# Attention by hash buckets and experts on one Trainium2 core: GpSimd's residuals wait for more of VectorE's subtractions, and the projection's table is loaded first

## The chip, the cores and the metric

The kernel runs on one core of a Trainium2 chip. The metric is the device time of one execution in microseconds (us). Engines are named as the profile names them: PE is TensorE (PEld its weight loads), DVE is VectorE, ACT is ScalarE, POOL is GpSimd, SP is SyncE, which here only issues DMAs. ACTq and SPq are the queues of DMA issues on ACT and SP.

## The reference

Four batches, eight heads, 768 positions, 64 channels per head. Each query and key gets a six-bit bucket from the signs of a projection, and a query attends only to keys of its bucket. Then each batch's 128 best rows by a gate score go through one expert.

```python
q_bits = (np.einsum('bhsd,dk->bhsk', q, proj) > 0)
k_bits = (np.einsum('bhsd,dk->bhsk', k, proj) > 0)
mask = q_bucket[:, :, :, None] == k_bucket[:, :, None, :]
scores = np.where(mask, scale * np.matmul(q, k.transpose(0, 1, 3, 2)), -1e9)
attn = np.exp(scores - max) ; attn = attn / (attn.sum(-1) + 1e-9)
x = (attn @ v) with the heads side by side, per batch [768, 512]
# expert: scores = x @ w_gate; the top 128 rows of each batch:
h = np.maximum(xe @ w1, 0.0)
out[b, top_idx] = xe + sigmoid(scores) * (h @ w2)
```

## The kernel before, in words

There are 32 heads (4 batches of 8), handled one after the other in a pipeline, and 16 pairs of heads, since a 128-partition tile holds two heads of 64 channels. Every number is kept as a high part in 16 bits and a low part, the residual, also in 16 bits, so that matrix products in 16-bit types come out near float32.

For a pair, `load_x` brings queries and keys (tiles X), `split_xh` (ACT) writes the high part into the tile T, `split_xl` (DVE, L500) the low part, and SP moves halves of T into the operands A and B of the two heads. `hash_half` multiplies X by the projection's table `pjt` (PE, L463) for two pairs at a time, `signs` turns the result into plus and minus values on DVE (L480), writes them to the tile `sg`, and then takes the difference of its two halves (L487; GpSimd for the first group, DVE for the seven others). SP moves the signs into A too. `load_v`, `split_vh` (ACT, L548) and `split_vl` (DVE, L554) do the same for the values: the low part of V. For the very last head, `score_v`, `score_vh` and `score_vl` (DVE, L576, 128x6 elements) add a column to V that makes its gate score; `sum_v`, `sum_lo` (DVE, L615) and `seed` make sums of V that start each head's accumulator.

For a head, `max_unit` (PE, L669), `max_relu` (ACT, L677) and `max_red` (DVE, L686, tiles mj and M) find each query's largest bucket match, 12 products of 128x384 per head in four PSUM banks that are handed round (`pmax.take`, `pmax.give`): a bank comes free when the engine that reads it is done. `st_unit` (PE, L720 with A and L724 with B) makes nine tiles of scores, `st_exp` (ACT, L738 and L740) their exponentials P in float32. The residual of P, tile R, is `r_chunk`: of the three key groups of a head, GpSimd takes group 1 in even heads, groups 0 and 2 in odd heads (L758, 128x1536 elements, 46 of them), and DVE the others in halves (L755, 128x768, 100 of them). `av` (PE, L774) multiplies high part and residual of P by V: for each of 36 blocks two weight loads of P and one of R. `recip` and `norm` (DVE, L784 to L796) divide.

The expert's weights are loaded and split between all this: ACT casts (L833), GpSimd subtracts (L835, 128x512, 16 of them). Expert products are L992 and L1016, their inputs turned by L957 and split by L965 and L1006.

The order of all of it is written out by hand: the table ORDER lists, one number per step, which step emits its instructions next. Each engine runs its own instructions in that order and waits on semaphores for what it needs from others. Besides these waits for data, there is one of another kind. A step on DVE that is wrapped in `mine` notes itself as the last one that used the path to SBUF which DVE and GpSimd share; a GpSimd step wrapped in `turn` waits, when it is emitted, until the DVE instruction noted at that moment is done. All 62 of GpSimd's residuals and weight subtractions (46 and 16) are wrapped in `turn`. On DVE L500, L563, L659, L755 and L857 are wrapped in `mine`; L487, L554 and L576 are not.

```python
    def mine(i):
        st["port"] = i
```

At the start `init_first` (L290) issues the first loads: half of the last pair's keys on ACT's queue (L292), of its queries on SP's queue (L293), and the table `pjt`, 128 rows of 276 bytes, on ACT's queue (L294). These become head 0. `negate` (ACT, L389) changes the sign of some columns of the table, `split_first` (ACT, L392) writes the high parts, `hash_first` (PE, L400) the projection, and the signs follow on ACT (L415, L416) and DVE (L410). `keep_warm` (PE, L311) issues products whose result nobody reads.

Of the kernel before, what the change touches and what calls it, by code (L numbers as in the profile page):

```python
# [16 lines left out]
ALU = mybir.AluOpType  # L17
# [226 lines left out]
def body(ctx, tc, qk, v, pj, wg, w1, w2, cst, out):  # L244
    nc = tc.nc
# [15 lines left out]
    pjt = cp.tile([P, PJW], F32, name="pjt")  # L261
# [27 lines left out]

    def init_first():  # L290
        xa = sb.tile([P, 2, S], F32, tag="P", name="Xa", bufs=4)
        nc.scalar.dma_start(xa[D:P, 1], qk[NP - 1, 1][D:P])  # L292
        nc.sync.dma_start(xa[D:P, 0], qk[NP - 1, 0][D:P])  # L293
        nc.scalar.dma_start(pjt, pj)  # L294
        nc.vector.memset(oneb, 1.0)
        nc.scalar.activation(oneb, oneb, AF.Copy)
        nc.gpsimd.memset(ones16, 1.0)
        nc.vector.memset(AA[0][0:D].bitcast(F32), 0.0)
        st["xa"] = xa
# [59 lines left out]
    def mine(i):  # L359
        st["port"] = i  # L360
# [9 lines left out]
    def need(*keys):  # L370

        assert all(k in st for k in keys), keys
# [97 lines left out]
    def signs(g, e):  # L470
        hp = st["hp", g, e]
        if ("sg", g) not in st:
            st["sg", g] = sb.tile([P, S // 2 + S], F16, tag="sg", name=f"sg{g}", bufs=2)
        if g > 1:
            need(("ps", 4 * g - 4))
        for j in range(2):
            st["sgd", 2 * g + j, e] = True
        t = st["sg", g]
        sd, sg = t[:, : S // 2], t[:, S // 2 :]
        nc.vector.tensor_scalar(  # L480
            sg[:, e * 384 : (e + 1) * 384], hp[:, :384], pjt[:, 66:67], pjt[:, 67:68],
            op0=ALU.is_gt, op1=ALU.mult,
        )
        pmax.give(f"hp{g}_{e}")
        if e:
            eng = nc.vector if g else nc.gpsimd
            eng.tensor_tensor(sd, sg[:, 0:384], sg[:, 384:768], op=ALU.subtract)  # L487

    def split_xh(p, r):
        if ("T", p) not in st:  # L490
# [59 lines left out]
    def split_vl(pr):  # L550
        need(("vh", pr))
        st["vl", pr] = True
        t, vv = st["V", pr], V[pr % NV].rearrange("p c h d -> p (c h) d")
        nc.vector.scalar_tensor_tensor(  # L554
            vv[:, :, VL : VL + D], t.rearrange("p c h d -> p (c h) d"), VS, vv[:, :, :D],
            op0=ALU.mult, op1=ALU.subtract,
        )

    def score_v():
        need(("vh", NH // 2 - 1))  # L560
# [12 lines left out]

    def score_vl():
        need("gvh")
        nc.vector.scalar_tensor_tensor(  # L576
            V[VLAST][:, :, 1, VL + D + 1 : VL + OW], st["gv"], VS, V[VLAST][:, :, 1, D + 1 : OW],
            op0=ALU.mult, op1=ALU.subtract,
        )
        st["gvl"] = True  # L580

    def sum_v(g):
# [634 lines left out]
    def begin():  # L1217
        init_first()
        keep_warm(0, WARM[0])
        negate()  # L1220
        split_first(1)
        split_first(0)
        low_first(1)
        hash_first()
        keep_warm(1, WARM[1])
# [15 lines left out]
    for g in range(NH // 4):  # L1241
        for e in range(2):
            at(hash_half, g, e)
            at(signs, g, e)
    for fn in (score_v, score_vh, score_vl):
        at(fn)
# [4 lines left out]
    for h in range(NH):  # L1251
# [15 lines left out]
        if h % 2 == 0:  # L1267
            for fn in (load_v, split_vh, split_vl):
                at(fn, h // 2)
            g, k = GROUP[h // 2]  # L1270
            if k == len(SUMS[g]) - 1:
                for fn in (sum_v, sum_hi, sum_lo, seed_row, seed_keep):
                    at(fn, g)
# [92 lines left out]
```

## Time and profile before

| | |
|---|---|
| median of 3 runs | 395.42 us (393.97 to 396.38) |
| the profiled execution | 395.86 us, of which the span of instructions is 393.8 us |
| PE busy | 376.2 us, 96% of the span |
| DVE busy | 346.6 us, 88% |
| ACT busy | 313.8 us, 80% |
| POOL busy | 180.0 us, 46% |
| mean granted clock of TensorE | 0.986 |

The span is counted from the first to the last instruction; times in the rows are from its start. Busy means that the engine has an instruction under way, even where that instruction itself stands and waits for a path to memory: such a stall lengthens the instruction's row and leaves no idle time. A row of the timeline gives start, duration, engine, line, operation, and in brackets the idle time before it with what ended it. Neighbouring rows of one engine overlap by up to 0.1 us, since each counts its own filling and draining.

### The profile page before, as it was taken

What the parts mean: (1) busy time and instruction counts of PE and PEld (TensorE: products, weight loads), DVE (VectorE), ACT (ScalarE), POOL (GpSimd) and SP (SyncE); (2) the same over time, 40 slices, a digit from 0 to 9 for tenths busy, and PEclk for the clock granted to TensorE, in tenths of its full rate; (3) what the DMA queues carried; (4) which work ended last, traced back from release to release, by engine and by line L of the source; (5) the groups of instructions that cost most, each with busy time, mean ns of one, the idle gap of its engine ahead of it and who ended that gap; (6) DMA issues with size and microseconds to landing.
All of it is one profiled execution on the core that took longest, in us unless ns stands there. A gap on an engine that the chain in (4) does not pass through costs nothing.

```text
span 393.8 us, 14144 instructions
## 1 busy us (share of the span) xinstructions
PE 376.2 (96%) x5736; PEld 274.5 (70%) x5746; DVE 346.6 (88%) x935; ACT 313.8 (80%) x665; POOL 180.0 (46%) x103
## 2 busy tenths in 40 slices
PE   6789999999999999799999999999999999899995
PEld 4346777677666777488657777676677788577894
DVE  3889999999799989979899899999999989989742
ACT  6899999899898998778588889988988986665210
POOL 8135567574736265724434444444326364220113
PEclk8799999999999999989999999999999999999999
DMA  7477667676776554633745543757464433010311
GB/s 236 139 196 230 176 197 221 181 220 165 221 206 166 138 156 125 199 95 106 233 117 185 142 132 91 204 148 199 100 173 110 103 67 112 2 42 2 108 30 53
DMA packets 26353, 56.37 MB, mean 143 GB/s; under 512 B 4218, under 2 KB 10942, under 8 KB 26288
## 3 DMA queue, kind: packets, MB, share of 16 engines
q1 hardware_dynamic: 15792, 36.89, 35.7%
q10 hardware_dynamic: 9824, 16.49, 12.9%
q0 software_dynamic: 672, 2.10, 1.7%
q8 instruction: 45, 0.74, 0.8%
q14 instruction: 20, 0.16, 0.1%
HBM read 26.58 MB, written 7.35 MB: 86 GB/s over the span
## 4 chain that ended last, share of the span: by engine, by line
PE 73%; DVE 9%; issue 7%; ACT 5%; DMA 2%; POOL 1%; POOLq 0%; ACTq 0%; SPq 0%; DVEq 0%
PE av L774 23%; PE st L720 14%; PE bank L669 14%; PE st L724 13%; PE bank L992 3%; DVE mj L686 2%; PE bank L463 2%; PE bank L1016 2%; ACT me L677 2%; DMA A<-sg 2%; DVE R L755 1%; DVE V L554 1%; ACT P L738 1%; DMA pjt<-in_pj_dram 1%; DVE sg L487 1%
## 5 line engine op out<-in xcount | busy, mean ns | idle before, releaser
L758 POOL TENSOR_TENSOR R<-P 128x1536 f16<-128x1536 f32 x46 | 134.2, 2919 | 136.4 <-ACT P L738 24.2
L774 PEld LDWEIGHTS <-P 128*128 128x128 bf16 x2304 | 126.3, 98 | 26.2 <-issue 0.8
L774 PE MATMUL av<-V,P 128*128 128x65 f16 (+2 forms) x2304 | 133.6, 193 | 0.1
L774 PE MATMUL av<-V,R 128*128 128x65 f16 (+1 forms) x1152 | 126.7, 193 | 0.0
L738 ACT ACTIVATE P<-st 128x512 f32<-128x512 f32 x192 | 111.8, 598 | 17.6 <-PE av L774 9.3
L720 PE MATMUL st<-A 128*128 128x512 f16 (+1 forms) x384 | 119.5, 326 | 1.4 <-ACT P L738 1.2
L724 PE MATMUL st<-B 128*128 128x512 f16 (+1 forms) x384 | 118.9, 326 | 0.7 <-ACT B L432 0.7
L686 DVE CUSTOM_DVE_ANT_0 mj<-bank,me 128x384 bf16<-128x384 f32 x192 | 102.4, 550 | 18.1 <-ACT me L677 9.0
L669 PE MATMUL bank<-A 128*128 128x384 f16 x384 | 108.7, 330 | 7.7 <-DVE W L615 2.0
L774 PEld LDWEIGHTS <-R 128*128 128x128 f16 x1152 | 106.2, 98 | 0.0
L677 ACT ACTIVATE me<-bank 128x384 f32<-128x384 f32 x192 | 92.2, 491 | 17.5 <-DVE M L686 8.0
L755 DVE TENSOR_TENSOR R<-P 128x768 f16<-128x768 f32 x100 | 94.1, 960 | 0.5 <-ACT P L738 0.2
L740 ACT ACTIVATE P<-st 128x512 f32<-128x512 f32 x96 | 56.9, 596 | 2.2 <-PE st L724 0.7
L669 PEld LDWEIGHTS <-A 128*128 128x128 f16 x384 | 34.8, 98 | 25.1 <-issue 5.6
L724 PEld LDWEIGHTS <-B 128*128 128x128 f16 x384 | 37.6, 98 | 18.0 <-issue 2.5
L720 PEld LDWEIGHTS <-A 128*128 128x128 f16 x384 | 37.5, 98 | 15.8 <-issue 2.5
L500 DVE SCALAR_TENSOR_TENSOR T<-X,T 128x768 f16<-128x768 f32 x32 | 31.6, 997 | 0.0
L493 ACT ACTIVATE T<-X 128x768 f16<-128x768 f32 x32 | 26.6, 841 | 0.6 <-DMA B<-T 0.6
L835 POOL TENSOR_TENSOR w2l<-W,w2h 128x512 bf16<-128x512 f32 x8 | 11.2, 1400 | 17.8 <-DVE R L755 12.5
L835 POOL TENSOR_TENSOR w1l<-W,w1h 128x512 bf16<-128x512 f32 x8 | 13.0, 1630 | 12.7 <-ACT w1h L833 6.5
L554 DVE SCALAR_TENSOR_TENSOR V<-V,V 128x768 f16<-128x768 f32 x16 | 17.8, 1114 | 0.3 <-ACT V L548 0.2
L796 DVE TENSOR_TENSOR x<-av,rc 128x384 f32<-128x384 f32 x32 | 17.7, 553 | 0.2
(142 smaller groups left out, 412.8 us busy)
## 6 DMA issues: line engine op xcount, KB each, us to landing
X<-in_qk_dram SPq DMA_DIRECT2D x32, 384.0 KB
B<-T SPq DMA_DIRECT2D x62, 192.0 KB
A<-T SPq DMA_DIRECT2D x31, 240.0 KB
V<-in_v_dram ACTq DMA_DIRECT2D x16, 384.0 KB
out_dram<-x ACTq DMA_DIRECT2D x6, 768.0 KB
W<-in_w_dram ACTq DMA_DIRECT2D x8, 512.0 KB
sbc<-scores SPq DMA_DIRECT2D x3, 384.0 KB
A<-sg SPq DMA_DIRECT2D x31, 31.5 KB
```

Source lines behind the costliest of these rows:

```text
L493: nc.scalar.activation(st["T", p][:, o : o + S], st["X", p, r], AF.Copy, scale=XS)
L500: mine(nc.vector.scalar_tensor_tensor(t[:, o : o + S], st["X", p, r], XS, t[:, i : i + S], op0=ALU.mult, op1=ALU.subtract))
L669: nc.tensor.matmul(pt[:, :384], a[0][:, t * P : (t + 1) * P], a[1][:, 384:768] if i else K[h % NA], start=True, stop=True,)
L677: nc.scalar.activation(me, st["mx", h, t, 0][:, :384], AF.Relu)
L686: nc.vector.tensor_tensor_reduce(out=jk, in0=st["mx", h, t, 1][:, :384], in1=st["me", h, t], op0=ALU.add, op1=ALU.max, scale=1.0 / MS, sca ...
L720: nc.tensor.matmul(pt[:, o : o + n], a[1][:, c * P : (c + 1) * P], a[0][:, q0 : q0 + n], start=True, stop=False,)
L724: nc.tensor.matmul(pt[:, o : o + n], bt[:, 0, c * P : (c + 1) * P], bt[:, 1, q0 : q0 + n], start=False, stop=True,)
L738: nc.scalar.activation(pp[:, r, 0:512], pt, AF.Exp, scale=ES)
L740: nc.scalar.activation(pp[:, :, 512:768], pt.rearrange("p (a b) -> p a b", a=2), AF.Exp, scale=ES)
L755: mine(nc.vector.tensor_tensor(t[:, r], pp[:, r], hi_view(pp, r), op=ALU.subtract))
L758: turn(nc.gpsimd.tensor_tensor(t, pp, hi_view(pp, a), op=ALU.subtract))
L774: nc.tensor.matmul(o[:, t, :n], l, vv[:, c, hh, v0 : v0 + n], start=False, stop=last and l is lo, skip_group_check=True,)
```

## The change

Three DVE instructions are wrapped in `mine` as well: the difference of the signs (L487), the low part of V (L554) and the low part of the last head's score column (L576). A GpSimd instruction wrapped in `turn` that is emitted after one of them now waits for it. And the table `pjt` is loaded by SP's queue, ahead of all else on it, where ACT's queue loaded it as its second. ORDER is the same.

```diff
     def init_first():
         xa = sb.tile([P, 2, S], F32, tag="P", name="Xa", bufs=4)
+        nc.sync.dma_start(pjt, pj)
         nc.scalar.dma_start(xa[D:P, 1], qk[NP - 1, 1][D:P])
         nc.sync.dma_start(xa[D:P, 0], qk[NP - 1, 0][D:P])
-        nc.scalar.dma_start(pjt, pj)
...
         if e:
-            eng = nc.vector if g else nc.gpsimd
-            eng.tensor_tensor(sd, sg[:, 0:384], sg[:, 384:768], op=ALU.subtract)
+            if g:
+                mine(nc.vector.tensor_tensor(sd, sg[:, 0:384], sg[:, 384:768], op=ALU.subtract))
+            else:
+                nc.gpsimd.tensor_tensor(sd, sg[:, 0:384], sg[:, 384:768], op=ALU.subtract)
...
-        nc.vector.scalar_tensor_tensor(
+        mine(nc.vector.scalar_tensor_tensor(
             vv[:, :, VL : VL + D], t.rearrange("p c h d -> p (c h) d"), VS, vv[:, :, :D],
             op0=ALU.mult, op1=ALU.subtract,
-        )
+        ))
...
-        nc.vector.scalar_tensor_tensor(
+        mine(nc.vector.scalar_tensor_tensor(
             V[VLAST][:, :, 1, VL + D + 1 : VL + OW], st["gv"], VS, V[VLAST][:, :, 1, D + 1 : OW],
             op0=ALU.mult, op1=ALU.subtract,
-        )
+        ))
```

Following `mine` and `turn` through ORDER, 14 of the 62 GpSimd instructions find another DVE instruction noted than before. For ten of them it is one that neither they nor a GpSimd instruction ahead of them waited for: the weight subtraction before R_0_1609, and the residuals R_0_2085, R_2_2668, R_0_3552, R_2_3713, R_0_5115, R_0_5596, R_1_5964, R_1_6369 and R_0_7649 (the last number only tells tiles apart). R_2_2668 and R_2_3713 get to wait for a difference of signs, R_0_7649 for the score column, the seven others for a low part of V. The order on PE, DVE and POOL is the same row by row, but for line numbers, which grow by two.

SP's queue at the start, before and after (A_90 and Xa belong to head 0, X to the next pairs):

```order
L1359 UNCONDITIONAL_BRANCH
L293 DMA Xa<-in_qk_dram 64x768
L378 DMA X_1_163<-in_qk_dram 128x768
L378 DMA X_0_165<-in_qk_dram 128x768
L378 DMA X_1_167<-in_qk_dram 128x768
```

```order
L1361 UNCONDITIONAL_BRANCH
L292 DMA pjt<-in_pj_dram 128x69
L294 DMA Xa<-in_qk_dram 64x768
L378 DMA X_1_163<-in_qk_dram 128x768
L378 DMA X_0_165<-in_qk_dram 128x768
L378 DMA X_1_167<-in_qk_dram 128x768
```

The table has come in front of every load of SP's queue, and all of them stand one place later.

POOL's waits around R_2_2668, before and after (semaphores of other engines by name; DVE_49 is VectorE's, Pool_49 GpSimd's own, DMAHW1_49 a load's):

```order
L835 TENSOR_TENSOR w2l<-W_2328,w2h 128x512 [waits DMAHW1_49,DVE_49,Activation_49]
L758 TENSOR_TENSOR R_0_2618<-P_0_2497 128x1536 [waits DVE_49,Activation_49]
L758 TENSOR_TENSOR R_2_2668<-P_2_2489 128x1536 [waits Activation_49,Pool_49]
L835 TENSOR_TENSOR w2l<-W_2328,w2h 128x512
L758 TENSOR_TENSOR R_1_2826<-P_1_2759 128x1536 [waits DVE_49,Activation_49,Pool_49]
```

```order
L837 TENSOR_TENSOR w2l<-W_2328,w2h 128x512 [waits DMAHW1_49,DVE_49,Activation_49]
L760 TENSOR_TENSOR R_0_2618<-P_0_2497 128x1536 [waits DVE_49,Activation_49]
L760 TENSOR_TENSOR R_2_2668<-P_2_2489 128x1536 [waits DVE_49,Activation_49,Pool_49]
L837 TENSOR_TENSOR w2l<-W_2328,w2h 128x512
L760 TENSOR_TENSOR R_1_2826<-P_1_2759 128x1536 [waits DVE_49,Activation_49,Pool_49]
```

R_2_2668 now also waits for DVE. At most of the ten places DVE_49 stood there before, and only the count that is waited for has grown.

DVE's rows around the score column, where R_0_7649 and R_2_7679 run on POOL (the same before and after; V_96<-gv is the score column, V_96<-V_6538 the last pair's low part):

```order
L686 ISA mj_2_7624,M_85<-bank_67,me_2_7514 128x384
L686 ISA M_85 128x1
L576 SCALAR_TENSOR_TENSOR V_96<-gv,V_96 128x6
L686 ISA mj_3_7651,M_85<-bank_67,me_3_7626 128x384
L686 ISA M_85 128x1
L796 TENSOR_TENSOR x_6636<-av_7423,rc_7606 128x6x64
L686 ISA mj_5_7677,M_85<-bank_64,me_5_7426 128x384
L686 ISA M_85 128x1
L554 SCALAR_TENSOR_TENSOR V_96<-V_6538,V_96 128x12x64
```

R_0_7649 now waits for the third row. The last row is emitted after both residuals, so neither waits for it, before or after.

## Rows read from the trace of the kernel before

**Rows 1.** The page's first part: busy time of each engine

```profile
PE 376.2 (96%) x5736; PEld 274.5 (70%) x5746; DVE 346.6 (88%) x935; ACT 313.8 (80%) x665; POOL 180.0 (46%) x103
```

**Rows 2.** Waits of PE: engine, line, waited for: us in total, times, longest

```profile
PE bank L669 <- DVE W L615: 2.0, 1, 2.0
...
PE bank L669 <- DVE M L686: 1.7, 2, 1.2
```

**Rows 3.** The page's part 5 (first row), then a source view: ns min/median/max

```profile
L500 DVE SCALAR_TENSOR_TENSOR T<-X,T 128x768 f16<-128x768 f32 x32 | 31.6, 997 | 0.0
...
L487 DVE TENSOR_TENSOR sg<-sg x7: 358/477/2845, 43.3 to 285.8; 128x384 f16<-128x384 f16 x7
```

**Rows 4.** Timeline of DVE, 162 to 167 us: start, duration, instruction

```profile
163.59 2.85 DVE L487 TENSOR_TENSOR sg<-sg 128x384 f16<-128x384 f16 x1
166.36 0.48 DVE L615 SCALAR_TENSOR_TENSOR W<-WH,cs,bank 128x260 f16<-128x260 f16 x1
```

**Rows 5.** Timeline of POOL, whole span

```profile
118.26 5.57 POOL L758 TENSOR_TENSOR R<-P 128x1536 f16<-128x1536 f32 x2 [3.05 <-DVE rc L784]
123.79 1.16 POOL L835 TENSOR_TENSOR w2l<-W,w2h 128x512 bf16<-128x512 f32 x1
...
163.48 2.74 POOL L758 TENSOR_TENSOR R<-P 128x1536 f16<-128x1536 f32 x1
...
261.93 2.77 POOL L758 TENSOR_TENSOR R<-P 128x1536 f16<-128x1536 f32 x1 [3.68 <-ACT P L738]
...
332.01 2.75 POOL L758 TENSOR_TENSOR R<-P 128x1536 f16<-128x1536 f32 x1 [5.58 <-DVE rc L784]
336.10 2.75 POOL L758 TENSOR_TENSOR R<-P 128x1536 f16<-128x1536 f32 x1 [1.34 <-ACT P L740]
```

**Rows 6.** Windows: stretch, us, busy of PE, PEld, DVE, ACT, POOL, clock, DMA share

```profile
164.86:166.89 2.03, 0.00 (x0) 0.00 (x0) 1.98 (x2) 0.51 (x2) 1.36 (x1) 1.00 0.81 237
168.04:171.45 3.41, 3.41 (x29) 2.70 (x28) 2.89 (x9) 2.45 (x6) 0.00 (x0) 0.50 0.39 127
171.45:175.00 3.55, 3.55 (x78) 3.24 (x76) 2.64 (x5) 3.00 (x8) 1.20 (x1) 1.00 0.02 5
```

**Rows 7.** Timeline of DVE, 330 to 341.5 us

```profile
333.49 1.31 DVE L576 SCALAR_TENSOR_TENSOR V<-gv,V 128x6 f16<-128x6 f32 x1
334.71 0.55 DVE L686 CUSTOM_DVE_ANT_0 mj<-bank,me 128x384 bf16<-128x384 f32 x1
...
336.13 3.54 DVE L554 SCALAR_TENSOR_TENSOR V<-V,V 128x768 f16<-128x768 f32 x1
```

**Rows 8.** Timeline of PE, 338 to 342 us

```profile
340.20 0.32 PE L669 MATMUL bank<-A 128*128 128x384 f16 x1 [1.21 <-DVE M L686]
340.80 0.38 PE L1016 MATMUL bank<-w2h,hth 128*128 128x512 f16 x1 [0.28 <-DVE htl L1006]
```

**Rows 9.** Timeline of all engines and DMA queues, 0 to 14 us

```profile
0.75 0.56 ACTq L292 DMA_DIRECT2D Xa<-in_qk_dram  x1
0.75 0.58 SPq L293 DMA_DIRECT2D Xa<-in_qk_dram  x1
...
1.35 0.60 ACTq L294 DMA_DIRECT2D pjt<-in_pj_dram  x1
...
4.95 0.22 ACT L389 ACTIVATE pjt<-pjt 128x18 f32<-128x18 f32 x1 [1.47 <-DMA pjt<-in_pj_dram]
5.19 1.57 ACT L392 ACTIVATE A<-Xa 64x768 f16<-64x768 f32 x2
```

**Rows 10.** Timeline of DVE, 118 to 126 and 261 to 262.2 us

```profile
120.73 0.49 DVE L487 TENSOR_TENSOR sg<-sg 128x384 f16<-128x384 f16 x1
...
123.87 1.89 DVE L500 SCALAR_TENSOR_TENSOR T<-X,T 128x768 f16<-128x768 f32 x1
...
261.14 0.96 DVE L554 SCALAR_TENSOR_TENSOR V<-V,V 128x768 f16<-128x768 f32 x1 [0.16 <-ACT V L548]
```

**Rows 11.** Timeline of PE's weight loads, 337.5 to 343 us

```profile
338.42 0.10 PEld L774 LDWEIGHTS <-R 128*128 128x128 f16 x1
```

## The prediction

> **What bounds the kernel now.** I read the page's busy times first: PE works 376.2 of 393.8 us [rows 1], so whatever shortens the kernel must remove idle time of PE or lie ahead of its first or behind its last product. Then the waits of PE, which say what its idle time is for. Apart from the start two rows stand out [rows 2]: 2.0 us in one piece before a product of L669, ended by DVE's L615, and 1.7 us in two pieces before L669, ended by DVE's L686. None of the fourteen rows of that view names a residual of GpSimd. So DVE is late in a few places, and the question is why.
>
> The source views answer it. The difference of signs takes 358 ns at best and 2845 ns at worst [rows 3]. The long one runs from 163.59 to 166.44, and GpSimd's residual from 163.48 to 166.22 [rows 4, 5]: it began 0.11 us earlier, and DVE's instruction ended just after it. DVE stood for it, 2.49 us. L615 follows it, and the bank that L615 reads is the one for which PE waits: in 164.86 to 166.89 PE does nothing. From 168.04 to 171.45, after that idle time, the granted clock is 0.50, 1.2 instead of 2.4 GHz, with PE busy throughout; before and after it is 1.00 [rows 6].
>
> The same is seen near the end. The score column begins at 333.49 under a residual that began at 332.01, and takes 1.31 us [rows 5, 7]. The residual had 1.27 us to go, so at most that is standing. At 336.13 the last pair's low part of V begins, 0.03 us after the next residual, and takes 3.54 us where another low part took 0.96 [rows 5, 7, 10]: 2.58 us. PE then idles 1.21 and 0.28 us for DVE [rows 8].
>
> **The change part by part.** Nothing is computed more or less. The sum is made against the profiled execution, 395.86 us, which is 0.44 us above the median of the runs, 395.42.
>
> *The sign difference at 163.59.* R_2_3713 will wait for it. It then takes its 0.36 us and ends at 163.95, and L615 at about 164.4, before PE comes to the product that needs it (164.86). The 2.03 us of idle time go. If the half clock goes with them, PE does the work of 3.41 us in half the time, 1.70 us less. Both together are 3.7, the first alone 2.0. Between them DVE decides: its own work after L615 is only released by PE's product, so it gains 2.0 us there, and in the window of the half clock it is busy 2.89 of 3.41 us [rows 6], so it can make up 0.5 us in that window and 0.9 (3.55 less 2.64) in the next, and 3.4 us is all it can have gained by 175 us. I take 3.1, between this and the 2.0. What is put behind the wait: R_2_3713 starts at about 164.1 (0.16 us from DVE's end to GpSimd's start, an estimate from the places where GpSimd waits for DVE now) instead of 163.48, and ends at 166.9. PE needs it first at 171.06 now, by counting its weight loads in the list of instructions; with 3.7 us less that is 167.4. Nobody waits. If the cover were gone, the price is the 0.6 us by which it ends later. Behind it on GpSimd stands a weight subtraction at 173.8 that waits for DVE anyway.
>
> *The score column and the last low part.* R_0_7649 will wait for the score column. DVE then does L576 at 333.49 in some 0.1 to 0.2 us, the three instructions that took from 334.71 to 336.13 in 1.42 us, and comes to the low part at about 335.0. The residual starts at about 333.8 and has the path until 336.55, so the low part still stands, but for this residual: it ends at about 337.5 instead of 339.67. That rests on the low part going ahead of the next residual, which has its exponentials at 336.0 and is queued behind the first. There is a row for this: two residuals back to back took 5.57 us instead of twice 2.74, and the sign difference that came at 120.73, inside the first one, got through between them with 0.49 us [rows 5, 10]. With the low part 2.1 us earlier both idle times of PE [rows 8] go: 1.5 us. The bounds are 0 (PE meets another wait at once) and 1.9 (with two gaps of 0.1 to 0.2 us beside them). R_0_7649 ends 1.8 us later, at 336.6; PE loads it first at 338.42 [rows 11], so 1.8 us are left. R_2_7679 ends at about 340.1 instead of 338.85, against a first use at 342.3 now and 340.8 with PE ahead by 1.5. Covered, by 0.5 us.
>
> The Trainium skill, SBUF — State Buffer, section "Who interferes with whom", says that of a VectorE instruction with two SBUF inputs and a GpSimd instruction, whichever issues first has the shared pair for its whole length and the other blocks fully, and that issue order decides. The rows at 163.59 and 333.49 agree (2.85 and 1.31 us). It speaks against this place: the wait only exchanges the residual that the low part stands behind, and if GpSimd's second counts as issued first too, the place gains nothing. By it the sum is that of rival A, by the row at 120.73 the one below.
>
> *The other eight places.* At one, R_2_2668, the order may turn: it starts some 0.3 us later, and the weight subtraction behind it, now at 123.79, comes after DVE's L500 at 123.87, which there takes 1.89 us against a mean of 1.00 [rows 3, 5, 10]. PE's other idle time before L669, 0.5 us at 126, hangs on this [rows 2]. I take 0.2 of these 0.5; bounds 0 and 0.5. At the seven others, six with a residual and one with a weight subtraction, GpSimd had begun beside a low part that was nearly done and stood for its rest, or came just behind it. The largest shift is at 261.93: the low part ends at 262.10 [rows 10], the residual starts at 262.26, 0.33 us later [rows 5]. The first use in PE, counted as above, lies 1.0 to 2.1 us behind the end of these residuals, and 0.7 us behind R_2_2668. I cost them at nothing; without that cover they cost 7 x 0.33 = 2.3 us.
>
> *The table.* Now it is issued at 1.35 and ACT gets it at 4.95, after 1.47 us of waiting; ACT's L392 follows without a gap [rows 9]. Issued at 0.75 it should be there about 0.6 us earlier, if it takes as long. The queries' half on SP's queue is issued 0.58 us later; PE's first products need that too, ACT only for the second of its two L392. So ACT is ahead by 0.5 us and PE by little. ACT leads the start until its exponentials, so I take 0.4; the bounds are 0.6, and a loss of 0.6 where the queries' half takes the table's place as the last to come.
>
> Sum: 3.1 + 1.5 + 0.2 + 0.4 = 5.2 us; 395.86 - 5.2 = 390.7 us. I leave it there for the median and do not take off the 0.44 us, since in the spread of the runs (2.4 us) some may have met fewer of these stalls than the profiled one: they hang on 0.11 and 0.03 us.
>
> **Rivals.**
>
> A. *The last low part stays behind.* R_2_7679 takes the path directly after R_0_7649, at 336.55, and the low part stands until 339.3 and ends at 340.25, 0.6 us later than now. For it: both residuals are ready then. Against it: the row at 120.73. The term of 1.5 becomes a loss of 0.6: 390.7 + 2.1 = 392.8.
>
> B. *PE gains the idle time at 165 us but little more.* The clock falls anyway at another gap, or a wait on ACT, which is busy 2.45 of 3.41 us and 3.00 of 3.55 [rows 6], comes in place of DVE's. Then 2.0 instead of 3.1, and half of the late term: 395.86 - 2.0 - 0.8 - 0.2 = 392.9.
>
> C. *Slower: the residuals become late.* The timed runs seldom have the stalls, since these hang on hundredths, and the new waits do their work alone: R_0_7649 1.8 us later, the eight others 0.33 us each, 2.6 in all, and PE standing for each of them. 395.4 - 0.4 + 4.4 = 399.4. It is slower than before as soon as more than 0.4 us of the 4.4 come through. Against it: no wait of PE names a residual, and the smallest reserve is over twice the shift.
>
> D. *Everything comes through*: 0.6 + 0.5 + 3.7 + 1.9 = 6.7, 389.2 us, or 388.7 against the median.
>
> **How the numbers follow.** The forecast 0.52, with 389.6 to 391.9 for its own range; A 0.15, B 0.17, C 0.05, D 0.11. From 395.42, 1% is 3.95 us, about what a measurement of this kernel can tell from no change: faster is below 391.47. That holds for D, for four fifths of the forecast's case and a tenth of A and B: 0.11 + 0.42 + 0.03 = 0.56. Slower is C, 0.05, less the part of it that stays within 1%: 0.04. The rest, 0.40, is within 1%. The range runs from 388.6 (D) to 393.6 (above A and B) and leaves out C and the far ends, 2 in 10.
>
> **What would show it.** In the changed trace none of the seven sign differences on DVE takes over 1 us. PE has no idle time over 1 us between 25 and 360 us. The half clock at 168 us is gone. The score column takes under 0.3 us, and the last low part, some 1.5 us after it, takes about 2.5 us, not 3.5. ACT's L389 comes at 4.4 instead of 4.95. The prediction is wrong if a wait of PE for a residual (L758 before, L760 after) appears with more than 0.5 us, if the sign difference is short and PE idles at 165 us all the same, or if the idle time comes back elsewhere in the same length.

## The result, and the profile after

The changed kernel takes 389.66 us (median of 4 runs, 388.62 to 390.24), beside 395.8 us for the kernel before (4 runs, 393.97 to 396.38): a ratio of 0.985, 95% interval 0.981 to 0.9889. The forecast was 390.7 us, faster by over 1% with a chance of 0.56; that is how it came out. In a later job, with five runs, it took 390.12 us against 395.25, ratio 0.9868 (0.984 to 0.9897). Here and below the microseconds gained are differences of medians; the ratios with their intervals were taken from all runs of a job and need not be the quotient of two medians.

The profiled execution took 390.24 us with a span of 388.1 us; before it was 395.86 and 393.8. First the row of busy times, which answers to [rows 1]:

```profile
PE 375.6 (97%) x5736; PEld 273.9 (71%) x5746; DVE 344.5 (89%) x935; ACT 313.8 (81%) x665; POOL 180.4 (46%) x103
```

Each engine executes as many instructions as before. What went is above all idle time of PE: the span is 5.7 us shorter, PE's busy time only 0.6 us; DVE's is 2.1 us less, since standing counts as busy. The waits of PE (engine, line, waited for: us in total, times, longest), whose lines answer to [rows 2]; line numbers have grown by two:

```profile
PE st L722 <- ACT P L740: 1.2, 2, 1.0
PE wq L311 <- POOL ones L297: 1.0, 1, 1.0
PE bank L671 <- DMA A<-sg: 0.9, 2, 0.7
PE bank L671 <- DVE R L757: 0.9, 1, 0.9
```

The wait of L671 for L615 (now L617) is gone, and so is its wait for L686 (now L688); the one wait for L688 that is left is 0.6 us of L450 at 15 us, which was there before too (0.5 us). The longest piece left is 1.0 us. No row names L760, GpSimd's residuals.

The place at 163 us: DVE and POOL (start, duration, instruction, and what ended the idle time ahead of it), then the stretch that was idle and the one that had half clock before; compare [rows 4 to 6].

```profile
163.08 0.36 DVE L487 TENSOR_TENSOR sg<-sg 128x384 f16<-128x384 f16 x1
163.35 0.48 DVE L617 SCALAR_TENSOR_TENSOR W<-WH,cs,bank 128x260 f16<-128x260 f16 x1
```

```profile
163.58 2.75 POOL L760 TENSOR_TENSOR R<-P 128x1536 f16<-128x1536 f32 x1 [0.58 <-DVE sg L487]
```

```profile
163.60:167.00 3.40, 3.40 (x38) 2.40 (x37) 2.80 (x10) 2.66 (x6) 2.73 (x1) 1.00 1.00 326
167.00:170.00 3.00, 3.00 (x67) 2.74 (x65) 2.97 (x8) 3.00 (x9) 0.00 (x0) 1.00 0.31 94
```

The difference of signs takes 0.36 us where it took 2.85. The residual waits for it, and then takes 2.75 as ever. PE has no gap, and the clock stays at 1.00. Over all seven such differences (min, median, max in ns), and the low parts L502, against [rows 3]:

```profile
L487 DVE TENSOR_TENSOR sg<-sg x7: 357/443/604, 42.6 to 281.8; 128x384 f16<-128x384 f16 x7
```

```profile
L502 DVE SCALAR_TENSOR_TENSOR T<-X,T x32: 940/950/1421, 12.6 to 337.2; 128x768 f16<-128x768 f32 x32
```

Near 120 us the order has turned, as the prediction thought it might. GpSimd's weight subtraction now comes second and stands for a part of its 1.88 us (1.16 in [rows 5]); DVE's L502 takes 1.07 instead of 1.89 [rows 10]:

```profile
118.23 2.75 POOL L760 TENSOR_TENSOR R<-P 128x1536 f16<-128x1536 f32 x1 [3.05 <-DVE rc L786]
121.36 2.75 POOL L760 TENSOR_TENSOR R<-P 128x1536 f16<-128x1536 f32 x1 [0.38 <-DVE sg L487]
124.07 1.88 POOL L837 TENSOR_TENSOR w2l<-W,w2h 128x512 bf16<-128x512 f32 x1
```

```profile
123.85 1.07 DVE L502 SCALAR_TENSOR_TENSOR T<-X,T 128x768 f16<-128x768 f32 x1
```

Near the end, DVE's score column and last low part, and the two residuals of POOL in one row; compare [rows 7]:

```profile
329.46 0.18 DVE L578 SCALAR_TENSOR_TENSOR V<-gv,V 128x6 f16<-128x6 f32 x1
...
331.82 1.55 DVE L556 SCALAR_TENSOR_TENSOR V<-V,V 128x768 f16<-128x768 f32 x1
```

```profile
329.81 6.17 POOL L760 TENSOR_TENSOR R<-P 128x1536 f16<-128x1536 f32 x2 [7.40 <-DVE V L578]
```

The column takes 0.18 instead of 1.31 us, the low part 1.55 instead of 3.54. Of the 6.17 us, 2.75 are the first residual, until about 332.56. The low part, begun at 331.82, is then in hand, and it is the second residual that is late: 3.42 us. PE's idle times of [rows 8] are gone.

The start, all engines and queues, against [rows 9]:

```profile
0.75 0.39 SPq L292 DMA_DIRECT2D pjt<-in_pj_dram  x1
...
2.74 0.20 ACT L389 ACTIVATE pjt<-pjt 128x18 f32<-128x18 f32 x1
3.69 1.71 ACT L392 ACTIVATE A<-Xa 64x768 f16<-64x768 f32 x2 [0.75 <-DMA Xa<-in_qk_dram]
...
7.66 0.87 PE L671 MATMUL bank<-A 128*128 128x384 f16 x2 [0.50 <-DVE A L410]
```

L389 starts at 2.74, not 4.95. What waits next is L392, 0.75 us for the keys; it starts 1.5 us earlier than before, and PE's first product of L671 0.84 us (8.49 before).

**Where the time came from.** PE runs the same 5736 matrix products in the same order before and after, so the start of the k-th in one trace can be set against the k-th in the other. PE is ahead by 0.84 us at the first L671, 0.63 until 82 us, 0.31 from 83 on, 0.03 at 106, 0.64 at 126, 0.83 at 130, 3.00 at 167 (the idle time), 4.63 at 172 (the half clock), 4.32 at 266, 4.02 at 283 and 5.65 at 343 us, by the times of before. It is the list that the experiments had to explain, the losses too: 0.32 at 82, 0.28 at 106, 0.30 at 266 and 0.30 at 283.

### The profile page after: what moved, and what is told of

It is laid out like the page before. It is cut to its first block, busy times and chain, and to the rows that moved or that the text cites. A ratio compares the mean times of both kernels' runs of the same rounds, so it can differ in the third digit from the quotient of the medians.

```text
span 388.1 us, 14144 instructions
## 1 busy us (share of the span) xinstructions
PE 375.6 (97%) x5736; PEld 273.9 (71%) x5746; DVE 344.5 (89%) x935; ACT 313.8 (81%) x665; POOL 180.4 (46%) x103
## 4 chain that ended last, share of the span: by engine, by line
PE 73%; DVE 8%; issue 8%; ACT 4%; DMA 3%; POOL 2%; SPq 1%; POOLq 0%; DVEq 0%; ACTq 0%
PE av L776 23%; PE bank L671 13%; PE st L722 13%; PE st L726 13%; PE bank L994 3%; PE bank L463 2%; DMA A<-sg 2%; DVE R L757 2%; DVE mj L688 2%; PE bank L1018 2%; ACT me L679 1%; PE wq L311 1%; DMA B<-T 1%; DVE jks L813 1%; ACT P L740 1%
## 5 line engine op out<-in xcount | busy, mean ns | idle before, releaser
L760 POOL TENSOR_TENSOR R<-P 128x1536 f16<-128x1536 f32 x46 | 133.7, 2907 | 134.7 <-DVE R L757 19.0
L688 DVE CUSTOM_DVE_ANT_0 mj<-bank,me 128x384 bf16<-128x384 f32 x192 | 102.2, 550 | 16.4 <-ACT me L679 7.8
L671 PE MATMUL bank<-A 128*128 128x384 f16 x384 | 108.1, 329 | 3.4 <-DMA A<-sg 0.9
L679 ACT ACTIVATE me<-bank 128x384 f32<-128x384 f32 x192 | 92.3, 491 | 13.8 <-PE bank L671 5.4
L757 DVE TENSOR_TENSOR R<-P 128x768 f16<-128x768 f32 x100 | 96.8, 987 | 0.4 <-ACT P L740 0.2
L671 PEld LDWEIGHTS <-A 128*128 128x128 f16 x384 | 34.8, 98 | 22.1 <-issue 2.9
L502 DVE SCALAR_TENSOR_TENSOR T<-X,T 128x768 f16<-128x768 f32 x32 | 31.3, 988 | 0.0
L837 POOL TENSOR_TENSOR w2l<-W,w2h 128x512 bf16<-128x512 f32 x8 | 12.3, 1544 | 13.5 <-DVE R L757 4.9
L994 PEld LDWEIGHTS <-w1h 128*128 128x128 f16 x256 | 15.9, 98 | 2.1
```

Of the source, the lines that this page charges most:

```text
L502: mine(nc.vector.scalar_tensor_tensor(t[:, o : o + S], st["X", p, r], XS, t[:, i : i + S], op0=ALU.mult, op1=ALU.subtract))
L671: nc.tensor.matmul(pt[:, :384], a[0][:, t * P : (t + 1) * P], a[1][:, 384:768] if i else K[h % NA], start=True, stop=True,)
L679: nc.scalar.activation(me, st["mx", h, t, 0][:, :384], AF.Relu)
L688: nc.vector.tensor_tensor_reduce(out=jk, in0=st["mx", h, t, 1][:, :384], in1=st["me", h, t], op0=ALU.add, op1=ALU.max, scale=1.0 / MS, sca ...
L757: mine(nc.vector.tensor_tensor(t[:, r], pp[:, r], hi_view(pp, r), op=ALU.subtract))
L760: turn(nc.gpsimd.tensor_tensor(t, pp, hi_view(pp, a), op=ALU.subtract))
```

## The experiments

The theory: DVE stood behind a residual that had started a moment earlier, and this is what PE waited for; each kind of wait pays at the one place where such a stand was long. The main rival: the sum is right by chance, and the gain comes from elsewhere, the table or a clock that happens not to fall.

**One part alone, on the kernel before.** Signs:

```diff
-            eng.tensor_tensor(sd, sg[:, 0:384], sg[:, 384:768], op=ALU.subtract)
+                mine(nc.vector.tensor_tensor(sd, sg[:, 0:384], sg[:, 384:768], op=ALU.subtract))
```

> Only the wait for the seven sign differences, nothing else of the change. Theory (VectorE's sign difference stood behind one residual, PE idled for it, and the clock fell): the difference at 163.6 us takes 0.36 us, PE's 2.0 us of idle time and the half clock at 168 us are gone, R_2_2668 behind the sign difference at 120.7 lets L500 through at 123.9 (0.6 us): 4.0 to 4.4 us faster than before. The late stall (low part of V, 3.5 us) stays. Rival (each of the ten new waits brings its share by spreading the two engines' work): two of ten waits, some 1.2 us.

Measured: 391.61 us against 395.28 (ratio 0.9898, 0.9852 to 0.9944): 3.7 us, somewhat under the 4.0 expected, with an interval of some 2 to 6 us. PE's idle time at 165 us, the one at 126 and the half clock at 168 are gone; the late low part still stands, 3.54 us, and PE's 1.21 and 0.28 us with it:

```profile
331.87 3.54 DVE L556 SCALAR_TENSOR_TENSOR V<-V,V 128x768 f16<-128x768 f32 x1
```

The low parts of V:

```diff
-        nc.vector.scalar_tensor_tensor(
+        mine(nc.vector.scalar_tensor_tensor(
             vv[:, :, VL : VL + D], t.rearrange("p c h d -> p (c h) d"), VS, vv[:, :, :D],
```

> Only the wait for the low parts of V. Theory: none of the long stalls is behind a low part that a GpSimd instruction waits for, so nothing is gained; seven GpSimd instructions end 0.1 to 0.3 us later, and at two of them (262 and 282 us) that reaches PE: 0 to 0.7 us slower than before. Rival (share of each wait): seven of ten waits, 3.5 to 4 us faster.

Measured: 395.42 us over ten runs, ratio 1.0009 (0.9983 to 1.0035). By themselves these waits bring or cost nothing that shows; the interval reaches from 1.4 us lost to 0.7 us gained.

The score column:

```diff
-        nc.vector.scalar_tensor_tensor(
+        mine(nc.vector.scalar_tensor_tensor(
             V[VLAST][:, :, 1, VL + D + 1 : VL + OW], st["gv"], VS, V[VLAST][:, :, 1, D + 1 : OW],
```

> Only the wait for the score column. Theory: the column takes 0.18 us instead of 1.31, the last low part some 1.5 instead of 3.5, PE's idle times of 1.2 and 0.3 us near 340 go: 1.4 to 1.9 us faster; the stall and the half clock at 164 to 171 us stay. Rival: one of ten waits, 0.6 us.

Measured: 393.36 us over ten runs, ratio 0.9943 (0.992 to 0.9966): 1.9 us. Both late instructions of DVE are short with this edit alone, and the place at 163 us is as before:

```profile
163.70 2.85 DVE L487 TENSOR_TENSOR sg<-sg 128x384 f16<-128x384 f16 x1
...
333.02 0.18 DVE L576 SCALAR_TENSOR_TENSOR V<-gv,V 128x6 f16<-128x6 f32 x1
335.39 1.54 DVE L554 SCALAR_TENSOR_TENSOR V<-V,V 128x768 f16<-128x768 f32 x1
```

So the last low part, which no residual waits for in either kernel, is helped by the wait for another instruction, as the prediction had it.

The table:

```diff
+        nc.sync.dma_start(pjt, pj)
...
-        nc.scalar.dma_start(pjt, pj)
```

> Only the table's load first. Theory: ACT's L389 and the first product of L669 come 0.8 us earlier and the half clock at 7.6 us goes, 0.3 us of it are left by 100 us, and a move of signs into A that lands at 105.5 us whatever came before takes that away: within 0.3 us of before at the end, PE's idle time before 105.6 us 0.2 to 0.3 us longer. Rival: the 0.3 to 0.8 us come through to the end. In both the stalls at 163.6 and 336 us may fall otherwise, since they hang on 0.11 and 0.03 us.

Measured: 393.71 us over ten runs, ratio 0.9946 (0.9917 to 0.9975): 1.6 us, so that neither the theory (0.3 at most) nor the rival (0.8 at most) holds, and more than PE keeps of the start in that trace (0.2 us from 39 to 165 us). The rest of its profile's gain comes at 168 to 171 us, from 0.2 to 1.9 us, with no change near there: PE idles 2.03 us as before, but the half clock does not follow. Idle stretch and the stretch behind it, in this kernel and in the one with the score column's wait:

```profile
164.59:166.62 2.03, 0.00 (x0) 0.00 (x0) 1.98 (x2) 0.52 (x2) 1.37 (x1) 1.00 0.68 241
167.78:171.19 3.41, 3.41 (x63) 3.04 (x62) 3.33 (x10) 3.30 (x9) 0.00 (x0) 1.00 0.42 125
```

```profile
164.96:167.00 2.04, 0.00 (x1) 0.00 (x0) 1.99 (x2) 0.52 (x2) 1.37 (x1) 1.00 0.73 229
167.92:171.33 3.41, 3.41 (x22) 2.40 (x21) 3.21 (x11) 2.31 (x5) 0.00 (x0) 0.50 0.48 134
```

**All but one.** If the table's 1.6 us were partly the half clock that the sign waits remove too, it must be worth less beside them. The changed kernel with the table where it was (on ACT's queue it stands behind the keys' half, not the queries'):

> All three kinds of wait, but the table stays where it was, on ACT's queue behind the queries' half. Theory: the 1.6 us that the table gained alone were mostly the half clock at 168 us, which that version missed by a shift of 0.2 us and which the sign waits remove as well; only the 0.2 to 0.4 us that PE keeps of the start are the table's own. Then 389.9 to 390.1 us, 0.2 to 0.4 over the changed kernel. Rival: the table is worth 1.6 us by itself, wherever the rest stands: 391.2 to 391.4 us.

In the same job the changed kernel as it is, as the measure:

> The changed kernel as it is, once more, as the measure for the three kernels beside it. Expected 389.7 us (389.2 to 390.2), about 6 us under the kernel before.

Measured: 390.76 us without (390.13 to 391.14) and 390.12 with (389.12 to 391.2), five runs each: 0.6 us. The two sets of runs overlap (the difference of their means is 0.6 with a standard error of 0.4), so that the theory's 0.2 to 0.4 fits and the rival's 1.6 is unlikely but not excluded. The traces agree with some 0.6: at 60 us PE is 0.2 to 0.8 us ahead of the trace of before in the nine profiles with the table first, and 0.7 us behind to 0.1 ahead in the four others with it second; the means are 0.5 ahead and 0.2 behind. They also show that starts with the same instructions differ by half a microsecond.

Where the rest of the 1.6 us came from is not shown. In the job in which the table was measured alone, the nine runs of the kernel before with a mean granted clock of 0.998 or more, which leaves no room for a half clock of 3.41 us, have a median of 394.9 us, and the table's version is still 1.2 us under them. By this the half clock is worth some 0.4 of the 1.6, and not most of it.

The changed kernel without the waits for the low parts (the diff of the low parts, taken back), in two jobs:

> The changed kernel without the wait for the low parts of V. Theory (those waits only cost): 0.3 to 0.7 us faster than the changed kernel, some 389.1 us. Rival (the low parts need the wait, too): one or more low parts take over 2 us and the time is 390.5 us or more.

> The changed kernel without the waits for the low parts of V. Theory: those waits cost 0.3 to 0.5 us, by way of VectorE's instructions that then stand behind a later residual at 260 and 282 us: 389.2 to 389.4 us, 0.3 to 0.5 under the changed kernel in the same job. Rival: nothing that lasts; the two agree within 0.1 us.

Measured: 389.3 us (four runs, 388.81 to 389.46; ratio to before 0.9824, 0.9792 to 0.9856), then 388.9 (five runs, 388.02 to 389.07; 0.9825, 0.9799 to 0.9851). In the second job all five runs lie under all five of the changed kernel, 1.2 us by the medians, twice and more what the theory allowed. So the low-part waits do cost, in company.

The theory's path, VectorE behind a later instruction of GpSimd, is seen in the traces, but at 75 to 82 us and not at 260 and 282. GpSimd's weight subtraction, then DVE's product with the gate's weights (L813) and the residuals of L757, first in the changed kernel, then in the second trace without the low-part waits:

```profile
75.47 1.16 POOL L837 TENSOR_TENSOR w1l<-W,w1h 128x512 bf16<-128x512 f32 x1 [4.87 <-DVE M L688]
75.86 1.05 DVE L813 CUSTOM_DVE_ANT_0 jks<-x,wgt 128x256 bf16<-128x256 f32 x1
78.88 2.32 DVE L757 TENSOR_TENSOR R<-P 128x768 f16<-128x768 f32 x2
```

```profile
75.16 1.37 POOL L837 TENSOR_TENSOR w1l<-W,w1h 128x512 bf16<-128x512 f32 x1 [4.04 <-ACT w1h L835]
76.38 0.43 DVE L813 CUSTOM_DVE_ANT_0 jks<-x,wgt 128x256 bf16<-128x256 f32 x1
79.21 1.89 DVE L757 TENSOR_TENSOR R<-P 128x768 f16<-128x768 f32 x2
```

With the waits the subtraction starts 0.8 us later behind the residual ahead of it (4.87 us idle, not 4.04), L813 stands for it, L757 for the residual that follows, and PE's product of L671 at 82 us comes 0.3 us later. This holds in all seven profiles with the low-part waits (L813 1.05 to 1.07 us, PE 0.27 to 0.28 us later) and in none of the seven without (L813 0.43, no loss there). It is some 0.3 us of the 0.4 to 1.2; the rest has no place yet. At 260 us DVE's L661 does take 0.58 instead of 0.35 us, but PE waits for something else: see the next point.

**What stands at 262 us.** In the changed kernel PE idles 0.87 us there; in its second profile it does not, though DVE's instructions around it lie within 0.03 us of the first. PE and its weight loads of the first, then the weight load of the second:

```profile
261.86 0.13 PEld L671 LDWEIGHTS <-A 128*128 128x128 f16 x2 [0.96 <-DMA A<-sg]
```

```profile
261.89 0.48 PE L671 MATMUL bank<-A 128*128 128x384 f16 x2 [0.87 <-DVE R L757]
```

```profile
261.06 0.13 PEld L671 LDWEIGHTS <-A 128*128 128x128 f16 x2 [0.19 <-issue]
```

The profile puts PE's 0.87 us down to DVE's L757, but that ended at 261.46, and the weight load names a DMA. SP issued the move of T into A at 257.83 and 257.81 us in the two; by the trace's record of queue events its last packet (told from the others by the order of the issues) landed at 261.80 and 261.00, each time 0.09 us or less ahead of PE's product. So the wait is for a transfer that takes 3.2 to 4.0 us, and it has nothing to do with the low parts: it is there without them too (0.98 us in the first trace of the kernel without, 0.23 in its second) and in the kernel before (0.58).

**The transfer at 105 us.** PE waits there for another of A's transfers, issued about 99 us beside a store of the output. The first store was emitted earlier (step 363 of ORDER moved from place 723 to 640, some 10 us):

> The changed kernel with the first store of batch 0's result issued by ACT at about 88 us instead of 98 us; all else in the same order. Theory (the move of signs that lands at 105.5 us shares the DMA engines with this store and a load of V): it lands 0.5 us or more earlier, PE's 0.7 us of idle time before 105.6 us shrinks to 0.2 or less, and the kernel is 0.4 to 0.7 us faster than the changed one. Rival (the move is bound by something else, as the moves ahead of it on SP's queue): the idle time stays at 0.7 us and the time is the same.

Measured: 390.47 us (389.29 to 390.99), ratio 0.9855 (0.9817 to 0.9893). PE's 0.71 us of idle time ahead of 105.6 are gone, and PE is 0.5 us ahead of the changed kernel there, but by 127 us that is given back: the theory is right for the transfer and wrong for the time. The same with the low-part waits left out:

> As the one before, and the first store of the output is also emitted at about 88 us instead of 98, so that the load for which PE waits at 105 us has the queues for itself. Theory: with the low-part waits gone nothing takes the 0.5 us back that this gained at 105 us, and 0.3 of them reach the end: 388.9 to 389.1 us. Rival: it is given back at 126 us as in the earlier version with the store moved, and the time is that of the kernel without the low-part waits.

Measured: 388.81 us (388.44 to 388.87), beside 388.9 for the store in its place: nothing that lasts. The idle time at 105 us is not worth an edit, since PE meets its next limit soon behind it.

**The stand put back by hand.** The sign difference of the fifth group made eight times, and four times, instead of once (it writes the same values again):

```diff
-                mine(nc.vector.tensor_tensor(sd, sg[:, 0:384], sg[:, 384:768], op=ALU.subtract))
+                for _ in range(8 if g == 4 else 1):
+                    mine(nc.vector.tensor_tensor(sd, sg[:, 0:384], sg[:, 384:768], op=ALU.subtract))
```

> The changed kernel with the sign difference of the fifth group (163 us) made eight times instead of once: VectorE is kept 2.5 us longer there with no residual of GpSimd beside it. Theory (the length of VectorE's stay alone makes PE's idle time, and the idle time the half clock): PE idles about 2 us, a stretch of 3.4 us at 0.50 of the clock follows, and 3.5 to 4 us of the gain are lost. Rival (the clock fell for another reason): idle time of 2 us, no half clock, some 2.1 to 2.5 us lost.

> The same with four sign differences, 1.1 us longer. Theory: PE idles some 0.6 us, the clock stays at 1.00, 0.5 to 0.8 us lost. Rival: the clock falls here, too, 2 us or more lost.

Measured, one run each: 394.05 and 391.31 us, which is 3.8 and 1.1 us over the changed kernel's profiled execution: as expected for eight, and more than the 0.5 to 0.8 us for four. With eight, DVE is busy for 3.11 us with no residual beside it, and everything is back: PE idles 2.61 us, then half clock for 3.41.

```profile
163.02 3.11 DVE L488 TENSOR_TENSOR sg<-sg 128x384 f16<-128x384 f16 x8
166.05 0.48 DVE L618 SCALAR_TENSOR_TENSOR W<-WH,cs,bank 128x260 f16<-128x260 f16 x1
```

```profile
163.97:166.58 2.61, 0.00 (x0) 0.00 (x0) 2.38 (x7) 0.52 (x2) 0.31 (x1) 1.00 0.76 275
167.78:171.19 3.41, 3.41 (x30) 2.77 (x29) 3.07 (x9) 2.50 (x6) 1.24 (x1) 0.50 0.41 124
```

With four PE idles 1.03 us and the clock stays:

```profile
164.18:165.21 1.03, 0.00 (x0) 0.00 (x0) 0.94 (x3) 0.52 (x2) 0.31 (x1) 1.00 0.93 286
166.00:169.40 3.40, 3.40 (x62) 2.90 (x61) 3.32 (x10) 2.79 (x7) 1.65 (x1) 1.00 0.63 217
```

That VectorE's lateness at this one place is the cause is shown by this: it needs no residual, only some 2.7 us more.

## Why the prediction was right, term by term

| term | predicted | profile against profile | alone, or left out |
|---|---|---|---|
| signs at 163 us | 3.1 | 2.2 + 1.6 = 3.8 | 3.7 alone, with the next row |
| L500 near 124 us | 0.2 | 0.6 + 0.2 = 0.8 | |
| score column, last low part | 1.5 | 1.6 | 1.9 alone |
| table | 0.4 | 0.6 | 0.6 beside the rest, 1.6 alone |
| seven low-part waits | 0 | -0.3 (at 82 us) | 0 alone, 0.4 to 1.2 lost beside the rest |
| waits for transfers into A (106, 266 us) and B (283 us) | not named | -0.9 | |

The prediction's sum was 5.2 us, that of its profile 5.62 (395.86 less 390.24), the medians give 6.1 and 5.1 in two jobs. That the sum is so near is in part luck: the terms that it names brought 6.8 us, about the 6.7 of rival D, and 1.2 us of losses, which it had at nothing or did not name, took the total back to 5.6. The median of 389.66 lies nearer to D's 389.2 than to 390.7, that of the later job nearer to 390.7. Rival B's sum leaves out the table's 0.4; with it B is 392.5 us, and nothing else changes. Signs 3.7 and column 1.9, each alone, and table 0.6 beside the rest are 6.2, and the kernel with just these three gains 6.9 and 6.35 in two jobs (396.18 less 389.3, 395.25 less 388.9); with the table's 1.6 alone the sum would be 7.2.

*Signs.* The step was right: residual 0.11 us early, sign difference and L615 behind it, PE's 2.03 us, half clock. The size of 3.1 was a cap by DVE, put at 3.4. The cap was too tight. DVE starts L617 3.0 us earlier, not 2.0, as PE was already 0.8 ahead there, and then it fits its work into what is left: 2.97 of 3.00 us busy at 167 to 170. The upper bound of 3.7 was the better reading of [rows 6].

*The place near 124 us.* The order turned, and L502 took 1.07. The whole of PE's 0.45 us went, where 0.2 of 0.5 was taken, and PE is 0.8 us further ahead by 130 us. The weight subtraction that stands in its stead cost PE nothing that shows.

*Score column and last low part.* The mechanism held to the order on the path: the low part got through between two residuals. Two sizes were off and made up for each other: it came 2.4 us after the column, not 1.5, since DVE's next instruction then waited 0.76 us for ACT's L679, and took 1.55 us, not 2.5, so that it ended 3.9 us after the column's start, where 4.0 was forecast. The row of the stand at 120.73 [rows 10] was the right guide, and rival A falls. (The cover that the prediction gives for the second residual as 0.5 us is 0.7 by its own times, 340.8 less 340.1; PE waits for it in neither trace.) The Trainium skill, SBUF — State Buffer, section "Who interferes with whom", says that the one that issues first has the shared pair. The trace agrees if a residual queued behind another counts as issued when it starts: the low part, issued at 331.82, went first, and the second residual, 0.7 us later, stood for it.

*Table.* The gain was put right, the way to it was not. "If it takes as long" was the step that failed: as the first load of SP's queue the table was there for L389 by 2.74 us, 2.0 after its issue, where it had taken 3.6 as the second of ACT's. L389 is 2.2 us early, not 0.55. But then the keys are the last to come, and L392 gains 1.5; PE keeps 0.63 until 82 us.

*Seven low-part waits at nothing.* This step failed. The prediction asked whether PE would wait for the later residuals, and PE waits for none, as forecast; it did not ask which VectorE instruction would come next on the path and stand behind a GpSimd instruction that now starts later. In five traces with the waits nine VectorE instructions are 0.1 to 0.6 us longer than in the seven without, some 3 us in all, and PE loses 0.3 us of it at 82 us. Alone the edit is worth 0 within its interval, beside the others it costs 0.4 and 1.2 us by the medians. The profiles of the changed kernel's second job and of the version without these waits agree within 0.3 us all the way from 127 us on, but the first was 0.6 us ahead from its start, by chance, and lost that at 82 and 106 us; it is also the fastest of its five runs, and the other the slowest of its five. So 0.3 us of the loss has a place, and the rest has none.

*Of the signs that were named*, these held: no sign difference over 1 us (0.604), no idle time of PE over 1 us between 25 and 360 us (longest 0.87), no half clock at 168, column under 0.3. Two did not: L389's time and the low part's length. Rivals B and C fall: the gain at 165 us came with the half clock's, and no residual is late for PE.

## What to carry to other kernels

Where two engines share a path and one is near the bound, look for the few instructions of the near one that take a multiple of their kind's median, and find out what started a tenth of a microsecond earlier; let that one wait, and only there. A wait put on every instruction of a kind, for order's sake, may take back part of the gain: here two of the three kinds of wait carried it all, and the version without the third is the fastest, 388.9 us. Ask also what the instruction that now starts later will meet on the path, since it may stop another in its turn. And take each part away from the whole as well as measuring it alone: the table gained 1.6 us alone and some 0.6 beside the rest.

## What the runs showed of the hardware that was not expected

The half clock behind an idle time of PE is not a fixed price. After 2.03 to 2.04 us it followed in the profiles of the kernel before and of the score column's version, and not in the table's (2.03); after 2.34 us (low parts alone) it did not, after 2.61 it did. Granted clock then was 0.50 for 3.41 us, 1.2 instead of 2.4 GHz. The runs' mean clocks show that the kernel before is split in the same way. Of 41 runs in three jobs, 17 had a mean clock of 0.985 to 0.987, as the profiled one, and a median of 396.3 us; 14 had 0.998 or more and a median of 394.9. The mean clock does not tell which stretch was slow, so this is a hint, but 1.4 us fits the 1.7 that such a stretch costs. In the profiles a mean of 0.984 to 0.986 goes with half clock both at the start and at 168 us, 0.988 to 0.991 with that at the start alone, 0.998 and more with neither (the last microseconds apart, which had half clock in nearly all). The table's version had no run under 0.988 in ten, so it seems to miss the half clock at 168 us as a rule; why a shift of 0.2 us avoids it stays open.

At the start half clock cost little. In the changed kernel's second profile the clock was 0.50 from 7.14 us for 6.83 us, in its first it was 1.00; the same product of PE started at 14.07 and 14.11 us. The second had been 0.44 us ahead at its first L671, so up to 0.4 us may have gone in between, in which PE has idle times in both. The five runs of the kernel before with a mean clock of 0.988 to 0.990, by the above with half clock at the start, have the same median, 394.9 us, as the 14 with 0.998 or more.

The same transfer of 240 KB, issued at the same point of the program, took 3.2 us in one execution and 4.0 in another, and PE's idle time for it ran from less than 0.2 to 0.98 us over the profiles. A wait that the profile ascribed to VectorE was this one; the weight load's row gave it away.
